# Attention and a gated feed-forward on one core: another written order for the first 19 steps, and 13 casts on VectorE instead of ScalarE

## The chip, the cores and the metric

The kernel runs on one core of a Trainium2 chip. A core has TensorE (PE in the profile), which multiplies matrices into PSUM; VectorE (DVE), ScalarE (ACT) and GpSimd (POOL), which work elementwise; and SyncE (SP), whose queue issues the loads and stores. Each engine works off its own list of instructions in order, and semaphores make one wait for another. The metric is the device time of one execution in microseconds (us), the median of several runs; lower is better.

## The reference

Linear attention over 8 batches of 8 heads with 576 rows of 64 columns, and behind it two matrix products with a nonlinear step between them, all in float32:

```
q_s = softmax(q, over the 64 columns);  k_s = softmax(k, over the 576 rows)
kv  = k_s^T v            (64 x 64, for each batch and head)
x   = q_s kv             -> 4608 x 512
h   = x @ w_in           w_in is 512 x 2048 (float64 words in memory)
g   = h - tanh(h)
out = g @ w_out          w_out is 2048 x 512 (float64 words in memory)
```

## The kernel before

**Two parts for each number.** The products run on float32r operands, a shorter format that TensorE multiplies faster. So each operand is split into a high part (a cast to float32r: xh, gh, the first half of a weight's tile w) and the rest (a subtraction: xl, gl, the second half of w), and a product is three matmuls: high by high, rest by high, high by rest. The change's "casts to the array's format" are the high parts of weights and of g.

**Chunks and steps.** The 4608 rows are nine chunks of 512. For each chunk j and each of the 16 blocks f of the 2048 hidden columns there is a step: 12 matmuls make ph (line 568), and then

- u, t, vv and mk on ScalarE (a square, a tanh, another square and a mask, line 583),
- g, tt, gg and cp on VectorE (lines 589 to 602): they put together h - tanh(h), by a polynomial where h is small,
- gh, the cast of g (line 605, ScalarE), and gl = g - gh (line 608, POOL or VectorE).

Two steps later, 12 matmuls (line 651) multiply gh and gl with w_out's block into four PSUM tiles po; the third of each three reads gl.

The order of steps is: chunk 0 with blocks 0 to 7, chunk 1 with all 16, chunk 0 with blocks 8 to 15, then chunks 2 to 8. Step n has its own names: ph17 is the h block of step 17, chunk 1 and block 9; in listings with numbers it is ph1_9.

**Weights.** Each of the 32 weight blocks (i0 to i15 of w_in, o0 to o15 of w_out) comes as 64-bit words and is turned into two float32r parts: ld (load), cl (a clamp, VectorE, line 157), lo and pr (ScalarE, lines 164 and 161), st (VectorE, line 168, makes c), ca (the cast of c, line 175, ScalarE) and sub (c minus the cast, line 179, VectorE or POOL). All 32 blocks are made within the first 19 steps, beside their h work.

**Attention.** For batch b: k and v loaded (k, v), maxima over rows (km.a to km.d, VectorE, lines 247 to 253; pm, mx, mh, ml, pb bring them to a row and back through TensorE), ks and ke (subtract and exp), pk (matmuls, line 323), sl, rs, rc, kn (norm, giving kvs, line 344). For a tile pair of q: mq, qu, qe, sq, sa, sr (softmax parts, lines 408 to 427), qn (norm, line 447), pt and qs (transpose and copy out), px (matmuls, line 487), xh and xl (lines 506 and 508).

**What sets the order.** Up to step 19 a table of names, ORDER, is worked off in order: each name issues one or a few instructions on its engine, so the table fixes each engine's list for TensorE, VectorE, ScalarE, POOL and SP. A star behind a name gives the piece to VectorE; without one, qu, qn, gl and sub go to POOL. `warm` issues matmuls on an identity whose results nobody reads. From step 19 on a loop issues the steps, TensorE and SP in the loop's order, the others where the scheduler puts them.

```
        for name in ORDER.split():
            eng = (nc.vector,) if name[-1] == "*" else ()
            ...
            if not eng and name.rstrip("0123456789") in ("qu", "qn", "gl") or name[:3] == "sub":
                eng = eng or (nc.gpsimd,)
            ops[name](*eng)
```

Waits between engines follow from who reads and writes which tile. Tiles of ph and of g's parts have two buffers each (vv and mk one), so a later step can also wait for an earlier one to be done with a buffer.

Of the kernel before, what the change touches and what calls it, by code (L numbers as in the profile page):

```python
# [29 lines left out]


ORDER = """
vo0.1 q0 mq0 q1 k0.0 mq1 qu0 k0.1 km0.a qe0 sq0 qu1 k0.2 km0.b sa0 km0.c sr0 qe1 ld.i0 ld.i4
vo0.0 km0.d warm13 pm0 qn0 lo.i4 sq1 lo.i0 mx0 sa1 ld.i2 mh0 sr1 q3 v0.0 ml0 cl.i0 cl.i4 pr.i0
vo0.2 v0.1 v0.2 cl.i2 pr.i2 warm5 pb0 st.i0 pr.i4 ks0.0 ld.i1 ks0.2 lo.i2 qn1 ke0.0 ks0.1 mq3
pt0 qn2 st.i2 qu3* warm4 pt1 ke0.2 ke0.1 st.i4 pk0.0 pk0.1 pk0.2 q2 k1.2 qs0 ca.i0 sl0 rs0 cl.i1
qs1 pt2 ca.i2 qn3 vo1.0 rc0 qe3 lo.i1 kn0 ld.i3 vo1.2 pt3 ld.i5 sub.i2 sub.i0 sq3 qs3 k1.0 pr.i1
qs2 k1.1 mq2 warm2 px0 px2 warm10 xh0.0 xh0.1 st.i1 qu2 xh2.1 ld.o0 xl0.0 xl0.1 xh2.0 xl2.1
ca.i1 xl2.0 ld.o1 lo.i3 cl.i5 qe2 lo.i5 cl.i3 ca.i4 pr.i5 ph0 sa3 pr.i3 sub.i1 u0 ld.i6 sr3 m0
sq2 sa2 km1.a sr2 st.i3 km1.b g0 ld.i7 ph1 km1.c vv0 ca.i3 t0 cl.o0 gg0 u1 pr.o0 km1.d ld.o2 t1  # L40
lo.o0 tt0 cl.o1 vv1 lo.o1 cp0 st.o0 ph2 pm1 sub.i4 mx1 t2 g1 tt1 mh1 qn6 gg1 lo.i6 u2 ca.o0 ml1
st.i5 gh0 m1 vo1.1 v1.0 cp1 vv2 qn4 pt6 ld.i10 sub.i3 qs6 ca.i5 ph3 qn5 t3 gl0 gh1 sub.i5 pb1
ks1.2 ks1.0 m2 v1.1 ld.o3 tt2 gl1 ph4 ks1.1 lo.o2 pt4 g2 ke1.0 u3 ke1.2 cl.i7 gg2 qs4 cl.o2 tt3
ke1.1 u4 vv3 cp2 cl.i6 g3 pr.o1 ld.o5 ph5 st.o1 m3 pr.o2 lo.o3 ca.o1 v1.2 gg3 pr.i6 cl.o3 st.o2
pk1.0 ld.o4 lo.i7 cl.i10 sub.o1* ld.o10 t5 ld.i12 ca.o2 pt5 sub.o0 ld.o6 qs5 pk1.1 cp3 cl.o5 po0
qn7 gh2 pk1.2 sub.o2* st.i6 pr.i7 tt5 t4 sl1 gl2* ld.o12 po1 rs1 ca.i6 g4 sub.i6 tt4 cl.o4 pr.o3
vv4 st.i7 gg4 m4 pt7 cl.o10 lo.o5 gh3 po2 u5 rc1 ca.i7 gl3* qs7 lo.o4 cp4 g5 pr.o5 ld.o9 ph6 m5
pr.o4 kn1 ld.o7 st.o3 px4 cl.o6 vv5 gh4 cl.i12 st.o4 ca.o3 gg5 ca.o4 xh4.1 sub.o3* st.o5 gl4* u6
sub.i7 cp5 xl4.1 xh4.0 cl.o9 t6 ph7 u7 vv6 lo.o7 po3 xl4.0 tt6 t7 px6 ca.o5 gh5 g6 m6 xh6.0
ld.i9 xh6.1 ld.i13 pr.o6 pr.i12 gg6 sub.o4 xl6.0 xl6.1 lo.i10 lo.o6 ld.o8 po4 cl.o12 cl.o7  # L50
sub.o5* cp6 cl.i9 ld.i11 pr.o7 gl5 g7 ph8 st.o6 vv7 lo.i11 m7 ld.i15 tt7 gg7 po5 gh6 pr.i10 cp7
gl6* st.i10 u8 ca.o6 st.o7 ph9 ld.i14 ld.i8 sub.o6* lo.i12 vv8 gh7 g8 po6 pr.i9 t8 lo.i15 t9 u9
tt8 ca.o7 pr.o12 gg8 gl7* m8 sub.o7* vv9 lo.i9 po7.0 cl.i15 cl.i8 pr.i15 tt9 st.i12 cp8 ld.o15
cl.i13 lo.o10 ld.o11 po7.1 ld.o14 gh8 lo.i8 m9 st.i15 ph10 gl8* g9 cl.o15 ev.0 po7.2 cl.i14 sv.0
gg9 ca.i12 u10 cl.o8 cp9 ph11 cl.i11 ev.2 ev.1 t10 ca.i15 vv10 g10 po7.3 tt10 po8.0 m10 sub.i15
cl.o11 cl.o14 po8.1 pr.o10 gg10 t11 gh9 ev.3 u11 ca.i10 gl9* pr.o8 pr.i8 cp10 g11 po8.2 tt11
vv11 m11 sub.i12 ph12 lo.o12 st.o10 gg11 st.i9 sub.i10 ca.o10 t12 lo.o8 lo.o14 st.i8 po8.3 gh10
ph13 cp11 ca.i9 u12 m12 ld.o13 po9 ca.i8 lo.i14 t13 sub.i9* sub.o10* gl10* pr.i11 sv.3 tt12 vv12
g12 st.o12 gh11 gg12 ca.o12 u13 st.i11 pr.o11 gl11* po10 cp12 pr.o9 m13 sub.o12 tt13 vv13 ca.i11
ph14 pr.i14 lo.i13 g13 gg13 po11 sub.i8* u14 sub.i11* cp13 gh12 gl12* t14 st.o8 ph15 lo.o9  # L60
pr.o15 g14 sv.1 po12 m14 gh13 tt14 lo.o11 st.o9 vv14 ca.o8 ph16 gl13* gg14 pr.i13 u15 sv.2 vv15
pr.o14 st.o11 g15 cp14 gh14 t15 sub.o8 lo.o15 u16 po13 m15 gg15 tt15 vv16 t16 cp15 ca.o11 gl14
cl.o13 sub.o11 tt16 g16 ca.o9 st.i14 ph17 gg16 lo.o13 st.i13 gh15 po14 gl15* m16 ca.i14 cp16
ca.i13 u17 g17 ph18 t17 sub.i13* st.o14 vv17 gg17 gh16 ca.o14 tt17 sub.o14* sub.o9* u18 po15
gl16* t18 st.o15 tt18 po16 m17 pr.o13 ca.o15 vv18 st.o13 cp17 gh17 g18 sub.i14 gg18 m18 ca.o13
cp18 gl17* sub.o13* gh18 gl18* sub.o15*
"""


# [1 line left out]
def attn_moe_kernel(  # L71
# [71 lines left out]
    def split_weight(kind: str, f: int) -> dict:

        st = {}

        def words(n: int) -> bass.AP:
            return staged[kind, f].bitcast(U32).rearrange("p (n t) -> p n t", t=2)[:, :, n]

        def clamp():
# [1 line left out]
            nc.vector.tensor_scalar(hif, hif, HI_MAX, -HI_MAX, op0=ALU.min, op1=ALU.max)  # L157
# [8 lines left out]
        def shift():
            st["c"] = c = dec.tile([P, DM], U32, name=f"c_{kind}{f}", tag="c")
            nc.vector.scalar_tensor_tensor(  # L168
                c, words(1), 3, words(0), op0=ALU.logical_shift_left, op1=ALU.bitwise_or
            )  # L170

        def cast():
            del staged[kind, f]
            wt[kind, f] = w = wts.tile([P, 2, DM], F32R, name=f"w_{kind}{f}", tag=f"w{kind}{f}")
            nc.scalar.copy(w[:, 0], st["c"].bitcast(F32))  # L175

        def rest(eng):
            w = wt[kind, f]
            eng.tensor_tensor(  # L179
                w[:, 1], st["c"].bitcast(F32), w[:, 0].bitcast(F32), op=ALU.subtract  # L180
            )
# [391 lines left out]
    def h_parts(j: int, f: int) -> dict:  # L573

        st = {}

# [4 lines left out]
        def act(tag: str, src: str, fn, **kw):
            of = {"dt": kw.pop("dt", F32)} | ({"bufs": kw.pop("bufs")} if "bufs" in kw else {})
            nc.scalar.activation(new(tag, **of), st[src], fn, **kw)  # L583
# [8 lines left out]

        def tt():
            nc.vector.tensor_tensor(st["t"], st["ph"], st["t"], op=ALU.subtract)  # L594

        def gg():
            nc.vector.scalar_tensor_tensor(  # L597
                st["g"], st["vv"], PB, st["g"], op0=ALU.add, op1=ALU.mult
            )

        def cp():
            nc.vector.copy_predicated(st["g"], st["mk"], st["t"])  # L602

        def gh():
            nc.scalar.copy(new("gh", F32R), st["g"])  # L605

        def gl(eng):
            eng.tensor_tensor(  # L608
                new("gl", F32R), st["g"], st["gh"].bitcast(F32), op=ALU.subtract
            )  # L610
# [221 lines left out]
```

## Time and profile before

| | us |
|---|---|
| median of 3 runs (899.38 to 899.83) | 899.44 |
| the profiled execution | 902.51 |
| its span, first to last instruction | 900.7 |
| TensorE busy in the span | 874.9 |
| VectorE busy | 616.7 |
| ScalarE busy | 555.0 |
| GpSimd busy | 289.2 |

The profiled execution is one run with the profiler on; the span is its part from the first to the last instruction. In the rows of the profile, L12 is line 12 of the kernel, `out<-in` are the tiles written and read, `xN` counts instructions, and `<-DVE t L594` behind a number names what ended a wait. A time line's row begins with the start and the length in us. Matmuls are pipelined, so that one that shows 0.39 us can follow the one before after 0.23 us.

### The profile page before, as it was taken

What the parts mean: (1) busy time and instruction counts of PE and PEld (TensorE: products, weight loads), DVE (VectorE), ACT (ScalarE), POOL (GpSimd) and SP (SyncE); (2) the same over time, 40 slices, a digit from 0 to 9 for tenths busy, and PEclk for the clock granted to TensorE, in tenths of its full rate; (3) what the DMA queues carried; (4) which work ended last, traced back from release to release, by engine and by line L of the source; (5) the groups of instructions that cost most, each with busy time, mean ns of one, the idle gap of its engine ahead of it and who ended that gap; (6) DMA issues with size and microseconds to landing.
All of it is one profiled execution on the core that took longest, in us unless ns stands there. A gap on an engine that the chain in (4) does not pass through costs nothing.

```text
span 900.7 us, 13173 instructions
## 1 busy us (share of the span) xinstructions
PE 874.9 (97%) x5008; PEld 716.6 (80%) x5008; DVE 616.7 (68%) x906; ACT 555.0 (62%) x967; POOL 289.2 (32%) x246
## 2 busy tenths in 40 slices
PE   5899989999999999999999999999999999999997
PEld 5777778878778888888888888888888888888886
DVE  7999988957576767567656865866765566454444
ACT  4899986655555657555646565565656566556553
POOL 4631112433144324332333332332433233222221
PEclk8999999999999999999999999999999999999999
DMA  9983301040142202300140011301100020001001
GB/s 292 306 314 118 115 9 41 24 140 2 53 100 61 69 1 82 107 24 1 47 123 7 24 47 35 107 0 48 48 24 1 1 70 12 1 1 48 1 1 47
DMA packets 79775, 57.47 MB, mean 64 GB/s; under 512 B 14688, under 2 KB 72032, under 8 KB 79712
## 3 DMA queue, kind: packets, MB, share of 16 engines
q1 hardware_dynamic: 79712, 56.63, 20.5%
q8 instruction: 39, 0.64, 0.3%
q14 instruction: 24, 0.20, 0.1%
HBM read 46.14 MB, written 10.49 MB: 63 GB/s over the span
## 4 chain that ended last, share of the span: by engine, by line
PE 78%; DVE 12%; ACT 5%; issue 2%; DMA 2%; POOL 1%; SPq 0%; DVEq 0%; ACTq 0%; POOLq 0%
PE po L651 36%; PE ph L568 36%; PE pk L323 2%; PE px L487 2%; PE pt L461 1%; DVE g L589 1%; DMA k<-in_k_dram 1%; DVE t L594 1%; DVE g L597 1%; DVE g L602 1%; ACT gh L605 1%; ACT mk L583 1%; DVE c_o L168 1%; DVE raw_i L157 1%; DVE c_i L168 1%
## 5 line engine op out<-in xcount | busy, mean ns | idle before, releaser
L651 PE MATMUL po<-w_o,gh 128*128 128x512 f32 x1152 | 358.7, 392 | 0.3 <-DVE w_o L179 0.2
L568 PE MATMUL ph<-xh,w_i 128*128 128x512 f32 x1152 | 313.4, 394 | 4.7 <-DVE t L594 2.3
L608 POOL TENSOR_TENSOR gl<-g,gh 128x512 fp32r<-128x512 f32 x128 | 171.5, 1340 | 389.3 <-ACT gh L605 367.0
L568 PEld LDWEIGHTS ph<-xh,w_i 128*128 128x128 f32 x1152 | 213.5, 188 | 49.8 <-DVE t L594 2.8
L651 PEld LDWEIGHTS po<-w_o,gh 128*128 128x128 f32 x1152 | 214.8, 188 | 47.3 <-issue 1.5
L589 DVE SCALAR_TENSOR_TENSOR g<-u,ph 128x512 f32<-128x512 f32 x144 | 98.2, 682 | 209.1 <-ACT t L583 204.7
L651 PE MATMUL po<-w_o,gl 128*128 128x512 f32 x576 | 224.5, 390 | 0.2 <-DVE gl L608 0.2
L605 ACT CAST gh<-g 128x512 fp32r<-128x512 f32 x144 | 89.5, 622 | 176.3 <-DVE g L602 168.5
L568 PE MATMUL ph<-xl,w_i 128*128 128x512 f32 x576 | 155.1, 391 | 0.0
L583 ACT ACTIVATE u<-ph 128x512 f32<-128x512 f32 x144 | 86.1, 598 | 78.4 <-PE ph L568 78.2
L597 DVE SCALAR_TENSOR_TENSOR g<-vv,g 128x512 f32<-128x512 f32 x144 | 117.4, 816 | 18.3 <-ACT vv L583 7.9
L651 PEld LDWEIGHTS po<-w_o,gl 128*128 128x128 f32 x576 | 108.3, 188 | 23.5 <-DVE gl L608 0.7
L568 PEld LDWEIGHTS ph<-xl,w_i 128*128 128x128 f32 x576 | 108.1, 188 | 23.7 <-DVE xl L508 0.5
L602 DVE COPY_PREDICATED g<-mk,t 128x512 f32<-128x512 int32 x144 | 119.6, 830 | 3.4
L583 ACT ACTIVATE mk<-ph 128x512 int32<-128x512 f32 x144 | 86.4, 600 | 36.1 <-DVE g L589 34.2
L583 ACT ACTIVATE vv<-u,b_pa 128x512 f32<-128x512 f32 x144 | 104.8, 727 | 0.7 <-DVE g L597 0.6
L594 DVE TENSOR_TENSOR t<-ph,t 128x512 f32<-128x512 f32 x144 | 98.0, 681 | 6.7 <-ACT mk L583 5.9
L583 ACT ACTIVATE t<-ph 128x512 f32<-128x512 f32 x144 | 85.6, 594 | 3.0 <-DVE g L589 3.0
L447 POOL TENSOR_TENSOR qn<-q,sq 128x512 f32<-128x512 f32 x30 | 34.6, 1153 | 27.7 <-PE pt L461 13.4
L413 POOL TENSOR_TENSOR q<-q,mq 128x1024 f32<-128x1024 f32 x14 | 28.0, 2003 | 46.4 <-DVE mq L408 44.6
L408 DVE TENSOR_REDUCE mq<-q 128x16 f32<-128x1024 f32 x15 | 18.3, 1217 | 23.3 <-DMA q<-in_q_dram 23.3
L179 POOL TENSOR_TENSOR w_i<-c_i,w_i 128x512 fp32r<-128x512 f32 x12 | 18.3, 1529 | 39.1 <-ACT w_i L175 39.1
(94 smaller groups left out, 577.4 us busy)
## 6 DMA issues: line engine op xcount, KB each, us to landing
k<-in_k_dram SPq DMA_DIRECT2D x16, 512.0 KB, 5.5
raw_i<-in_moe_w_in_dram SPq DMA_DIRECT2D x16, 512.0 KB, 6.7
raw_o<-in_moe_w_out_dram SPq DMA_DIRECT2D x16, 512.0 KB, 8.3
...
```

The source lines that it names most:

```text
L179: eng.tensor_tensor(w[:, 1], st["c"].bitcast(F32), w[:, 0].bitcast(F32), op=ALU.subtract)
L413: eng.tensor_tensor(qf, qf, mq, op=ALU.subtract)
L447: eng.tensor_tensor(qn.rearrange("p a g d -> p g a d"), qt[:, :, j].rearrange("p (g a) d -> p g a d", g=2), sq[:, :, j : j + 1] .broadcast ...
L568: nc.tensor.matmul(ph, w[:, i, c], x[:, c, :], start=(n == 0), stop=(n == len(ops) - 1))
L583: nc.scalar.activation(new(tag, **of), st[src], fn, **kw)
L589: nc.vector.scalar_tensor_tensor(new("g"), st["u"], C2, st["ph"], op0=ALU.mult, op1=ALU.mult)
L594: nc.vector.tensor_tensor(st["t"], st["ph"], st["t"], op=ALU.subtract)
L597: nc.vector.scalar_tensor_tensor(st["g"], st["vv"], PB, st["g"], op0=ALU.add, op1=ALU.mult)
L602: nc.vector.copy_predicated(st["g"], st["mk"], st["t"])
L605: nc.scalar.copy(new("gh", F32R), st["g"])
L608: eng.tensor_tensor(new("gl", F32R), st["g"], st["gh"].bitcast(F32), op=ALU.subtract)
L651: nc.tensor.matmul(po[t], g[:, cols], wt["o", f][:, w], start=(begin and n == 0), stop=(end and n == 2),)
```

## The change

The code gets a helper `copy`, and `cast` and `gh` an engine argument, so that a star moves these two kinds of casts to VectorE; the lines below it move down by 3 or 4. ORDER is written anew: the same names, and one more `warm`. Its starred names are 46 instead of 31. One line of the table stands for all here.

```diff
 ORDER = """
-vo0.1 q0 mq0 q1 k0.0 mq1 qu0 k0.1 km0.a qe0 sq0 qu1 k0.2 km0.b sa0 km0.c sr0 qe1 ld.i0 ld.i4
...
+q0 mq0 k0.0 k0.1 qu0* km0.a vo0.0 qe0 k0.2 km0.b km0.c q1 vo1.1 q3 ld.i1 km0.d warm13 pm0 vo0.2
...
 """
...
+    def copy(eng, dst, src):
+        (eng.tensor_copy if eng else nc.scalar.copy)(dst, src)
+
...
-        def cast():
+        def cast(eng=None):
             del staged[kind, f]
             wt[kind, f] = w = wts.tile([P, 2, DM], F32R, name=f"w_{kind}{f}", tag=f"w{kind}{f}")
-            nc.scalar.copy(w[:, 0], st["c"].bitcast(F32))
+            copy(eng, w[:, 0], st["c"].bitcast(F32))
...
-        def gh():
-            nc.scalar.copy(new("gh", F32R), st["g"])
+        def gh(eng=None):
+            copy(eng, new("gh", F32R), st["g"])
```

On VectorE are now the casts of the weights i0, i9, i10, i11, i13, i14, o1, o2 and o7, and gh of steps 6, 7, 9 and 10. Of the other pieces that may be on either engine, VectorE has 15 gl as before, 16 sub (15 before), one qu (q0's; before it was that of the fourth q tile, q3) and one qn (none before); POOL has the others. Behind the planned part the lists of all engines hold the same instructions in the same order as before, save that some stand a place or two apart among their neighbours between steps 19 and 21.

Three places show how the lists move. The first is the start of VectorE's list, up to the first maxima of k. Before:

```order
L408 TENSOR_REDUCE mq0_0_114<-q0_0_112 128x16
L408 TENSOR_REDUCE mq0_1_120<-spare_q_116 128x16
L247 TENSOR_TENSOR km0_125<-k0_0_118 128x512
L421 TENSOR_REDUCE sq0_0_128<-q0_0_112 128x16
L250 TENSOR_TENSOR km0_125<-km0_125,k0_1_123 128x512
L424 TENSOR_SCALAR sq0_0_128<-sq0_0_128 128x16
```

and now:

```order
L412 TENSOR_REDUCE mq0_0_112<-q0_0_110 128x16
L417 TENSOR_TENSOR q0_0_110<-q0_0_110,mq0_0_112 128x1024
L251 TENSOR_TENSOR km0_119<-k0_0_114 128x512
L254 TENSOR_TENSOR km0_119<-km0_119,k0_1_116 128x512 x2
L257 TENSOR_TENSOR km0_119<-km0_119,kr0_124 64x512
L412 TENSOR_REDUCE mq0_1_158<-spare_q_128 128x16
```

The subtraction of q0's maxima (second row) came to VectorE, and the second q tile (spare_q) stands behind all of k's maxima; on SP's list its load moved behind those of k in the same way.

The second place is a moved cast, gh of step 9 (gh1_1: chunk 1, block 1), with its neighbours on VectorE. Before, when gh1_1 was on ScalarE's list:

```order
L157 TENSOR_SCALAR raw_o14_1126<-raw_o14_1126 128x512
L597 SCALAR_TENSOR_TENSOR g1_2_1190<-vv1_2_1188,g1_2_1190 128x512
L608 TENSOR_TENSOR gl1_1_1220<-g1_1_1150,gh1_1_1213 128x512
L602 COPY_PREDICATED g1_2_1190<-mk1_2_1200,t1_2_1184 128x512
L589 SCALAR_TENSOR_TENSOR g1_3_1225<-u1_3_1216,ph1_3_1167 128x512
```

and now:

```order
L598 TENSOR_TENSOR t1_2_1179<-ph1_2_1155,t1_2_1179 128x512
L601 SCALAR_TENSOR_TENSOR g1_2_1177<-vv1_2_1175,g1_2_1177 128x512
L134 CAST gh1_1_1225<-g1_1_1134 128x512
L606 COPY_PREDICATED g1_2_1177<-mk1_2_1189,t1_2_1179 128x512
L612 TENSOR_TENSOR gl1_1_1228<-g1_1_1134,gh1_1_1225 128x512
L161 TENSOR_SCALAR raw_i9_941<-raw_i9_941 128x512
```

The cast stands two places ahead of the gl that reads it, on the same engine.

The third place is the end of the planned part on VectorE, with gl of step 17 (gl1_9) and of step 18 (gl1_10). Before:

```order
L602 COPY_PREDICATED g1_9_1554<-mk1_9_1617,t1_9_1569 128x512
L589 SCALAR_TENSOR_TENSOR g1_10_1629<-u1_10_1584,ph1_10_1556 128x512
L597 SCALAR_TENSOR_TENSOR g1_10_1629<-vv1_10_1622,g1_10_1629 128x512
L602 COPY_PREDICATED g1_10_1629<-mk1_10_1633,t1_10_1600 128x512
L608 TENSOR_TENSOR gl1_9_1638<-g1_9_1554,gh1_9_1627 128x512
L179 TENSOR_TENSOR w_o13_1635<-c_o13_1624,w_o13_1635 128x512
L608 TENSOR_TENSOR gl1_10_1643<-g1_10_1629,gh1_10_1641 128x512
L179 TENSOR_TENSOR w_o15_1620<-c_o15_1602,w_o15_1620 128x512
```

and now:

```order
L606 COPY_PREDICATED g1_9_1584<-mk1_9_1586,t1_9_1550 128x512
L598 TENSOR_TENSOR t1_10_1595<-ph1_10_1567,t1_10_1595 128x512
L601 SCALAR_TENSOR_TENSOR g1_10_1618<-vv1_10_1604,g1_10_1618 128x512
L606 COPY_PREDICATED g1_10_1618<-mk1_10_1625,t1_10_1595 128x512
L183 TENSOR_TENSOR w_i13_1621<-c_i13_1602,w_i13_1621 128x512
L612 TENSOR_TENSOR gl1_10_1632<-g1_10_1618,gh1_10_1630 128x512
L183 TENSOR_TENSOR w_o15_1590<-c_o15_1557,w_o15_1590 128x512
L612 TENSOR_TENSOR gl1_9_1651<-g1_9_1584,gh1_9_1648 128x512
```

Step 17's gl is now the last of the planned part, behind step 18's and the sub of o15; the sub of o13 went to POOL's list.

More of the change, by code (lines that the diff above doesn't have):

```diff
@@ L32 @@
 ORDER = """
-vo0.1 q0 mq0 q1 k0.0 mq1 qu0 k0.1 km0.a qe0 sq0 qu1 k0.2 km0.b sa0 km0.c sr0 qe1 ld.i0 ld.i4
[L34 to L66, printed above, removed]
+q0 mq0 k0.0 k0.1 qu0* km0.a vo0.0 qe0 k0.2 km0.b km0.c q1 vo1.1 q3 ld.i1 km0.d warm13 pm0 vo0.2
+mq1 mx0 ld.i0 mh0 ml0 warm5 pb0 qu1 vo0.1 mq3 v0.0 warm10 sq0 cl.i1 sa0 lo.i1 v0.1 ks0.0 qe1
@@ new lines @@
+lo.i0 pr.i1 sr0 sq1 qu3 ke0.0 ks0.1 cl.i0 v0.2 ld.i4 sa1 qn1 qe3 ks0.2 ke0.1 warm4 pk0.0 sr1 pt1
+qn0 sq3 ke0.2 pk0.1 st.i1 pr.i0 qn3* sa3 pk0.2 lo.i4 cl.i4 sl0 ld.i3 qs1 ld.i2 rs0 qn2 pt0 pt3
+sr3 q2 rc0 warm3 pt2 pr.i4 qs0 ca.i1 kn0 cl.i3 ld.i5 st.i0 qs3 qs2 px0 xh0.0 sub.i1* k1.0 xh0.1
+ca.i0* px2 cl.i2 xh2.0 xh2.1 qn7 xl0.0 lo.i3 xl0.1 lo.i2 k1.1 xl2.0 xl2.1 pr.i2 sub.i0 k1.2
+pr.i3 warm2 pt7 warm2 ph0 lo.i5 mq2 st.i2 ph1 ca.i2 cl.i5 pr.i5 st.i4 ca.i4 st.i3 sub.i2* km1.a
+ca.i3 st.i5 u0 ld.o2 t0 g0 ca.i5 vv0 km1.b tt0 ld.o0 ld.o1 km1.c u1 gg0 m0 km1.d cp0 qn6 ph2 pm1
@@ new lines @@
+g1 mx1 t1 vv1 gg1 mh1 cl.o0 qu2 vo1.2 qe2 ld.i7 u2 ml1 lo.o0 sub.i3 sq2 gh0 tt1 ph3 cl.o1 m1 qs7
+vo1.0 lo.o1 sa2 pr.o0 vv2 pb1 lo.o2 v1.2 sub.i5 cp1 st.o0 sub.i4 pr.o1 t2 ph4 sr2 pt6 gh1 ks1.0
+ks1.1 v1.0 gl0 u3 m2 ke1.0 v1.1 ks1.2 ph5 t3 g2 tt2 ke1.1 qs6 pk1.0 ca.o0 gl1 qn4 ld.i6 ke1.2
+gg2 g3 vv3 ld.o3 cp2 ld.o6 tt3 pk1.1 st.o1 cl.o2 ca.o1* m3 u5 pt4 t5 ld.o4 gg3 ld.o5 pk1.2 sl1
+qs4 cl.i6 cl.o3 pr.o2 st.o2 u4 cl.i7 pr.i6 ca.o2* qn5 rs1 pr.o3 sub.o0 lo.i6 ld.i10 po0 gh2 pt5
+ld.o7 cl.o6 qs5 cp3 ld.o10 rc1 st.i6 kn1 gl2* sub.o2* cl.o5 ld.o8 cl.o4 lo.o3 t4 tt5 g4 ld.o11
@@ new lines @@
+sub.o1 tt4 po1 m4 ca.i6 ld.i12 gh3 pr.i7 pr.o4 st.o3 lo.i7 ld.i8 lo.o4 vv4 st.o4 gg4 ca.o3
+sub.i6 sub.o3* gl3* st.i7 px4 cp4 xh4.1 xh4.0 ca.o4 vv5 lo.o5 po2 ld.i15 ph6 pr.o6 xl4.1 u6
+xl4.0 ca.i7 g5 m5 lo.o6 ld.o9 sub.i7* gg5 gh4 st.o6 pr.o5 gl4* st.o5 po3 px6 cp5 ld.i9 xh6.0
+xh6.1 ph7 xl6.1 ld.i11 t6 ld.i13 ca.o5 m6 sub.o4 ca.o6 g6 tt6 lo.i12 gh5 xl6.0 po4 t7 gl5* vv6
+cl.o7 u7 lo.o7 ld.o12 cl.i10 cl.i12 gg6 cl.i8 ld.o13 lo.i8 cp6 tt7 pr.o7 gh6* g7 vv7 gg7 sub.o5
+gl6* lo.i15 ph8 st.o7 sub.o6 m7 cp7 po5 u8 ph9 ca.o7* vv8 gh7* lo.i9 gl7 pr.i8 t8 lo.o9 lo.i10
@@ new lines @@
+g8 pr.i12 m8 po6 u9 tt8 gg8 pr.i10 sub.o7* po7.0 cp8 ld.o14 cl.o8 cl.i11 po7.1 po7.2 t9 gh8
+st.i12 st.i8 lo.o12 gl8* ca.i8 g9 st.i10 lo.o8 cl.o13 pr.i11 ca.i10* po7.3 cl.i15 ev.2 vv9
+lo.i13 tt9 m9 ph10 cl.i13 gg9 cp9 u10 pr.o8 cl.o12 vv10 g10 t10 sub.i10* tt10 ev.3 po8.0 gg10
+m10 ph11 t11 po8.1 ph12 u11 gh9* cp10 gl9* cl.i9 ev.1 lo.o14 ev.0 g11 po8.2 m11 vv11 ld.i14
+ca.i12 lo.i11 st.o8 t12 tt11 gg11 pr.i9 tt12 ca.o8 cl.o14 pr.o12 po8.3 ph13 po9 gh10* lo.i14
+cp11 pr.o13 u12 cl.i14 cl.o10 cl.o9 sv.1 pr.o9 sub.i8 gl10* u13 sv.2 g12 st.i11 lo.o11 m12
@@ new lines @@
+sub.o8* sub.i12 gh11 vv12 st.o12 pr.o10 st.i9 po10 gg12 t13 ph14 cp12 m13 pr.i14 ca.i11* pr.i15
+gl11* vv13 ca.i9* ca.o12 g13 tt13 gh12 u14 sub.i9* gg13 sub.o12* pr.o14 po11 cl.o11 st.i15
+ld.o15 vv14 cp13 m14 gh13 st.o14 sv.0 t14 ph15 lo.o13 ca.i15 gl12* sub.i11 st.o9 gl13 tt14
+ca.o14 g14 lo.o15 t15 sub.i15* gg14 po12 pr.i13 ph16 cp14 u15 m15 vv15 st.o13 g15 gh14 ca.o13
+sub.o14 tt15 pr.o11 po13 u16 gl14* cl.o15 gg15 st.i14 g16 ph17 po14 lo.o10 ca.o9 sub.o9* t16
+ca.i14* cp15 pr.o15 vv16 st.o11 ca.o11 t17 u17 gh15 sub.i14* st.o15 tt16 gg16 m16 gl15* cp16
@@ L67 @@
+sub.o13 ph18 st.o10 vv17 g17 m17 gh16 ca.o15 ca.o10 gg17 t18 gl16* sub.o10* u18 st.i13 vv18 po15
+g18 tt17 ca.i13* cp17 tt18 m18 gg18 cp18 sub.i13* gh18 gl18* sv.3 sub.o15* po16 gh17 sub.o11
+gl17*
 """
```

## The prediction

> **What bounds the kernel now.** I read the page first, then the engines' busy time stage by stage, then the waits of TensorE (PE) and VectorE (DVE), and last the time lines at the places where they meet.
>
> ```profile
> PE 874.9 (97%) x5008; PEld 716.6 (80%) x5008; DVE 616.7 (68%) x906; ACT 555.0 (62%) x967; POOL 289.2 (32%) x246
> ```
>
> The page says TensorE, but a busy TensorE isn't one at its peak. The count of matmuls (the x) in equal stretches of 20 us tells more; the last three columns are the granted clock, the DMA share and GB/s.
>
> ```profile
> 40.00:60.00 20.00, 17.94 (x154) 14.40 (x155) 19.67 (x34) 18.27 (x33) 9.94 (x6) 1.00 1.07 363
> 60.00:80.00 20.00, 18.61 (x134) 14.29 (x134) 19.22 (x35) 18.91 (x38) 5.42 (x4) 1.00 0.24 83
> 80.00:100.00 20.00, 19.48 (x84) 15.24 (x83) 18.65 (x35) 19.19 (x37) 0.00 (x0) 1.00 0.41 150
> 100.00:120.00 20.00, 19.45 (x86) 15.74 (x86) 17.82 (x27) 18.38 (x35) 5.45 (x4) 1.00 0.37 119
> 120.00:140.00 20.00, 17.66 (x71) 14.11 (x70) 17.00 (x27) 17.45 (x33) 5.47 (x4) 0.91 0.00 0
> 140.00:160.00 20.00, 20.00 (x90) 16.54 (x89) 17.69 (x28) 12.10 (x23) 2.50 (x4) 1.00 0.21 47
> 400.00:420.00 20.00, 20.00 (x120) 16.25 (x119) 16.55 (x24) 12.12 (x21) 5.78 (x4) 1.00 0.10 27
> ```
>
> From about 140 us on TensorE is busy all the time. Up to there VectorE and ScalarE are 85 to 98% busy and TensorE waits for them now and then. So the planned part is bound by those two, the rest by TensorE, and **what the planned part gains or loses by its last step goes into the end one for one**. The waits confirm it: the longest one behind the start of the first h block is
>
> ```profile
> PE ph L568 <- DVE t L594: 2.3, 1, 2.3
> ```
>
> ```profile
> 134.94 4.33 PE ph L568 x12
> ...
> 142.32 2.72 PE ph L568 x12
> ```
>
> and behind it, in the chain of waits, twelve matmuls take 4.33 us where they take 2.72 a little later: the granted clock (0.91 in that stretch) fell with the wait. The point where VectorE hands over to TensorE is the product po, whose third matmul reads gl:
>
> ```profile
> 63.66 0.50 PE L651 MATMUL po<-w_o,gl 128*128 128x512 f32 x1 [0.22 <-DVE gl L608]
> ```
>
> ```profile
> 150.70 0.68 DVE L608 TENSOR_TENSOR gl<-g,gh 128x512 fp32r<-128x512 f32 x1
> ```
>
> ```profile
> 153.50 0.39 PE L651 MATMUL po<-w_o,gl 128*128 128x512 f32 x1
> ```
>
> (The first and the last row are TensorE's, the middle one VectorE's.) At 63.66 it waits. The gl of step 17, ready at 151.38, is read at 153.50: a slack of 2.1 us only. That step is my yardstick, since it is the last gl that VectorE makes in the changed order.
>
> **The change, part by part.**
>
> *Casts.* 13 casts leave ScalarE.
>
> ```profile
> L175 ACT CAST w_i<-c_i 128x512 fp32r<-128x512 f32 x16 | 10.1, 631 | 1.4 <-DVE c_i L168 1.4
> L605 ACT CAST gh<-g 128x512 fp32r<-128x512 f32 x144 | 89.5, 622 | 176.3 <-DVE g L602 168.5
> L179 DVE TENSOR_TENSOR w_o<-c_o,w_o 128x512 fp32r<-128x512 f32 x11 | 7.5, 685 | 0.8 <-ACT w_o L175 0.8
> ```
>
> ```profile
> 69.79 0.43 DVE L157 TENSOR_SCALAR raw_o<-raw_o 128x512 f32<-128x512 f32 x1
> 70.13 0.42 DVE L157 TENSOR_SCALAR raw_i<-raw_i 128x512 f32<-128x512 f32 x1
> 70.51 0.69 DVE L168 SCALAR_TENSOR_TENSOR c_o<-raw_o 128x512 uint32<-128x512 uint32 x1
> 71.12 0.69 DVE L597 SCALAR_TENSOR_TENSOR g<-vv,g 128x512 f32<-128x512 f32 x1
> ```
>
> ```profile
> 70.88 0.64 ACT L605 CAST gh<-g 128x512 fp32r<-128x512 f32 x1
> 71.39 1.17 ACT L175 CAST w_o<-c_o 128x512 fp32r<-128x512 f32 x2
> ```
>
> Instructions overlap, so the price is from start to start: a cast on ScalarE 0.51 us (70.88 to 71.39), thirteen 6.7 us. On VectorE no such cast of this size is in the trace. The nearest row with one input from SBUF is the clamp, 0.34 (69.79 to 70.13); the nearest with two is 0.61 (70.51 to 71.12). A cast has one input, so I take 0.34: 13 x 0.34 = **+4.4 us on VectorE**, at most 13 x 0.61 = 7.9. The Trainium skill, VectorE: DVE Perf Modes, section "The perf-mode tier table", gives fp32 copies out of SBUF twice the rate of two-input operations; the clamp row agrees, and at the single rate the sum would be the 7.9.
>
> *Two more pieces on VectorE.* One more sub (16 for 15) and one qn come from POOL: 2 x 0.61 = **+1.2**. qu takes part on VectorE for another q tile, once in either order.
>
> *Order at the end.* Before, three instructions of the planned part stood behind step 17's gl on VectorE (the gl of step 18, the subs of o13 and o15); now none does, all of VectorE's planned work is ahead of it: 3 x 0.61 = **+1.8**. Together 7.4 us more work stand ahead of the yardstick.
>
> *What hides it.* VectorE isn't full:
>
> ```profile
> 44.70:150.70 106.00, 97.75 (x162) 0.98 0.38 128
> ```
>
> ```profile
> DVE t L594 <- ACT mk L583: 4.1, 5, 2.2
> DVE w_i L179 <- ACT w_i L175: 1.4, 1, 1.4
> DVE w_o L179 <- ACT w_o L175: 0.8, 3, 0.4
> DVE t L594 <- ACT t L583: 0.7, 1, 0.7
> ```
>
> Of 106.00 us it idles 8.2, and these four waits for ScalarE are 7.0 of it. ScalarE loses 6.7 us, and four weights get cast and subtracted on VectorE alone. So I let 6.2 us of the idle time be filled and keep 2.0 (a cast whose result the next instruction reads costs some): **-6.2**, with bounds of 0 and -8.2. If this cover is gone, the 7.4 us are late in full.
>
> *Collisions.* A second loss is no idle time in the profile:
>
> ```profile
> 72.64 1.29 POOL L179 TENSOR_TENSOR w_o<-c_o,w_o 128x512 fp32r<-128x512 f32 x1 [3.32 <-ACT w_o L175]
> 72.69 1.80 DVE L168 SCALAR_TENSOR_TENSOR c_o<-raw_o 128x512 uint32<-128x512 uint32 x1
> ```
>
> ```profile
> 165.86 1.30 POOL L608 TENSOR_TENSOR gl<-g,gh 128x512 fp32r<-128x512 f32 x1 [1.84 <-issue]
> ```
>
> ```profile
> 165.92 1.26 DVE L268 CAST mh<-mx 128x4 fp32r<-128x4 f32 x1
> ```
>
> The c that takes 0.69 at 70.51 takes 1.80 beside a POOL operation, and a cast of four columns takes 1.26: VectorE is held until POOL has ended. The new casts can be held likewise. The Trainium skill, SBUF — State Buffer, section "Who interferes with whom", says so and speaks against this change: a cast or copy in the two-port mode and a GpSimd operation lock each other out, whole instructions long; the mh row agrees. In price: POOL is busy 16.3 of 80 us (60 to 140), so of 13 casts 2.7 would meet it and lose half of 1.3 us each, 1.7 us. Against it two POOL operations go, each worth up to 1.3 us. I take **0**, with bounds of -2.6 and +2.5.
>
> *The start.* The written order of the first 45 us changes most: k's tiles are loaded ahead of the second q tile, q0's subtraction is VectorE's, and the second batch's k comes earlier.
>
> ```profile
> 7.77 1.90 POOL L413 TENSOR_TENSOR spare_q<-spare_q,mq 128x1024 f32<-128x1024 f32 x1
> ```
>
> ```profile
> 7.81 2.41 DVE L247 TENSOR_TENSOR km<-k 128x512 f32<-128x512 f32 x1 [0.49 <-DMA k<-in_k_dram]
> ```
>
> ```profile
> 27.50 1.21 DVE L408 TENSOR_REDUCE mq<-q 128x16 f32<-128x1024 f32 x1
> 28.63 0.68 DVE L168 SCALAR_TENSOR_TENSOR c_i<-raw_i 128x512 uint32<-128x512 uint32 x1
> 29.23 2.47 DVE L508 TENSOR_TENSOR xl<-px,xh 128x512 fp32r<-128x512 f32 x4
> ```
>
> ```profile
> 30.77 1.17 PE L568 MATMUL ph<-xh,w_i 128*128 128x512 f32 x4
> 31.78 1.18 PE L568 MATMUL ph<-xl,w_i 128*128 128x512 f32 x4
> ```
>
> The first h block is held by the last xl, ended at 31.70. VectorE's work ahead of it changes by: + qn 0.61, + sub of i1 0.61, + cast of i0 0.34, + one clamp 0.34, - one row maximum of q 1.13 (27.50 to 28.63), - two c of 0.61: -0.5 us. The km that lost 1.8 us beside POOL at 7.81 is free of it now, as q0's subtraction is VectorE's, but mh and the clamps come to stand beside two q subtractions of 1.90 on POOL instead, with k1's maxima beside a third. I take **-0.7**, bounds -2.0 and +2.0.
>
> *Sum.* +4.4 +1.2 +1.8 -6.2 +0 -0.7 = +0.5: step 17's gl is ready at 151.9 instead of 151.4. Nothing says that TensorE must be where it was: before, it was pushed to 153.50 by the wait at 132 to 135 and the slow clock behind it. If VectorE is what it follows, it reads gl at once, at 151.9: 1.6 us before 153.50. All that follows (POOL's and ScalarE's work for the next batches, SP's loads behind the planned ones) stands in the same order as before, under a TensorE without gaps. The forecast is **-1.6 us**.
>
> **The rivals.**
> - *VectorE fills up* (slower). Its idle time is pinned to TensorE's h tiles and to short chains, so only 2.0 us instead of 6.2 close. For it: VectorE is the fuller of the two up to 80 us, and work goes to it. Against it: 7.0 us of idle are ScalarE's doing. +4.2: end +2.6, 902.0. It decides from 4.6 us of idle left: there the 2.1 us of slack are used up.
> - *Dear casts* (slower). At 0.61 each +3.5: end +1.9, and with half the price of the lock 902.2. Against it stands the clamp row.
> - *The start and the meetings with POOL go well* (faster). The start gives 2.0, collisions fall by 2.2: 3.5 better, end -5.1, 894.3. For it: km's 1.8 us are avoided. Against it: POOL's list is hardly shorter.
> - *It doesn't do what it says.* ScalarE's relief only makes ScalarE wait, VectorE's gaps and load cancel, and TensorE's waits stay: 899.4.
>
> **How the numbers follow.** The profiled execution took 902.51 us, 1.8 more than its span of 900.7, and is 3.1 above the median of the runs, 899.44. I carry the shift to the median: 899.44 - 1.6 = **897.9**. About 0.2% (1.8 us) is what a measurement here can tell from no change, so the bounds are 897.6 and 901.2. Forecast: chance 0.45, own range 895.5 to 900.5 (0.21 faster, 0.24 same). VectorE full: 0.22 (0.19 slower, 0.03 same). Dear casts: 0.07 slower. Start well: 0.18 faster. No effect: 0.08 same. Faster 0.39, same 0.35, slower 0.26. The range takes in the rivals' centres and a little more, 893.5 to 903.5; with several bounds at once (collisions +2.5 and no idle time filled, or the start -2.0, collisions -2.6 and all of it filled) it could be 906.6 or 892.0.
>
> **What would show it.** Right: casts on line L134 of VectorE start 0.34 apart from their followers; VectorE's idle time between 45 and 150 falls from 8.2 to about 2; step 17's gl ends near 152 and TensorE waits for it; the clock has no dip near 134. Wrong: VectorE still idles 5 us or more there; casts of 1 us and over beside POOL; the first h block later than 31.5; or TensorE waiting for something other than VectorE (a weight's cast on ScalarE, or a load) in that stretch.

## The result and the profile after

The changed kernel takes 909.56 us (median of 3 runs, 909.32 to 910.11) against 899.44 before: 1.0101 times as long, 95% interval 1.0087 to 1.0115. The forecast was 897.9, range 893.5 to 903.5. The profiled execution took 910.11 us with a span of 908.3, 7.6 more than before; the medians are 10.1 us apart, since the profiled execution of before lay 3.1 us above its median and this one 0.6. In the profiles TensorE is 7.6 us late from step 25 on (ph0_9, 196.0 instead of 188.4) and stays so to the end. At step 17's gl, in the last steps of the planned part, it is 8.4 us late (161.86 instead of 153.50): all of the loss is made there.

The page's line of busy times, and then the engines' busy time in stretches of 20 us (PE, PEld, DVE, ACT, POOL with counts; granted clock, DMA share, GB/s), of the changed kernel:

```profile
PE 880.2 (97%) x5018; PEld 719.3 (79%) x5018; DVE 623.8 (69%) x921; ACT 548.6 (60%) x954; POOL 286.6 (32%) x244
```

(TensorE has ten rows more than before because the new table has two more `warm` entries, `warm3` and a second `warm2`, and not one: five products of two rows each.)

```profile
40.00:60.00 20.00, 16.23 (x138) 13.43 (x139) 18.95 (x27) 14.68 (x26) 9.36 (x7) 0.83 1.00 361
60.00:80.00 20.00, 16.80 (x98) 12.09 (x96) 16.64 (x32) 15.38 (x29) 4.60 (x3) 1.00 0.61 218
80.00:100.00 20.00, 18.41 (x105) 14.33 (x103) 17.78 (x33) 17.85 (x33) 3.85 (x3) 1.00 0.09 27
100.00:120.00 20.00, 18.62 (x79) 14.53 (x80) 18.91 (x36) 17.13 (x32) 2.60 (x2) 1.00 0.25 80
120.00:140.00 20.00, 19.50 (x86) 15.85 (x85) 19.60 (x31) 16.62 (x31) 4.74 (x3) 1.00 0.21 60
140.00:160.00 20.00, 17.73 (x77) 14.01 (x76) 18.84 (x31) 12.71 (x24) 3.12 (x4) 1.00 0.21 47
```

Against the same stretches of before, VectorE did less between 40 and 80 us (35.6 us busy, 38.9 before) and ScalarE fell by 7.1 us (30.1, 37.2 before) where it gave away two casts, those of o1 and o2. In 60 to 80 us TensorE began 98 matmuls instead of 134. So the engines that bind this part stand idle where they had been full.

The prediction's yardstick, VectorE up to the end of step 17's gl: 151.38 us before, 161.80 now, where TensorE waits for it. The first row is VectorE's (time line of the changed kernel), the second TensorE's:

```profile
161.12 0.68 DVE L612 TENSOR_TENSOR gl<-g,gh 128x512 fp32r<-128x512 f32 x1
```

```profile
161.86 0.50 PE L655 MATMUL po<-w_o,gl 128*128 128x512 f32 x1 [0.68 <-DVE gl L612]
```

Split into busy and idle time, by VectorE's rows alone of the view of stretches (length of the stretch, busy time and count; then the granted clock, the DMA share and GB/s). Before:

```profile
20.00:44.70 24.70, 24.56 (x38) 1.00 0.93 302
44.70:151.40 106.70, 98.44 (x163) 0.98 0.38 127
```

and after:

```profile
20.00:44.70 24.70, 24.63 (x40) 0.94 0.83 263
44.70:161.80 117.10, 107.81 (x183) 0.98 0.37 126
```

The 10.4 us are 9.4 of busy time (98.44 to 107.81) and 1.0 of idle time (8.26 to 9.29). The prediction had 6.7 more busy time and 6.2 less idle time.

**Where VectorE idles now.** Its three costliest waits for others between 30 and 165 us (us in total, times, longest):

```profile
DVE c_o L172 <- ACT raw_o L168: 3.4, 1, 3.4
DVE t L598 <- ACT mk L587: 1.5, 1, 1.5
DVE t L598 <- ACT t L587: 0.9, 1, 0.9
```

The longest seen from both sides, in the time lines. ScalarE:

```profile
66.21 0.58 ACT L587 ACTIVATE t<-ph 128x512 f32<-128x512 f32 x1
70.33 0.60 ACT L587 ACTIVATE mk<-ph 128x512 int32<-128x512 f32 x1 [3.54 <-DVE t L598]
...
73.52 0.65 ACT L168 ACTIVATE raw_o<-raw_o 128x512 uint32<-128x512 uint32 x1
```

VectorE:

```profile
69.56 0.68 DVE L598 TENSOR_TENSOR t<-ph,t 128x512 f32<-128x512 f32 x1
70.16 0.68 DVE L172 SCALAR_TENSOR_TENSOR c_o<-raw_o 128x512 uint32<-128x512 uint32 x1
74.20 0.69 DVE L172 SCALAR_TENSOR_TENSOR c_o<-raw_o 128x512 uint32<-128x512 uint32 x1 [3.36 <-ACT raw_o L168]
```

ScalarE has t of step 4 done at 66.79 and could make the mask mk of the same step, but waits until VectorE's tt of step 4 has ended at 70.24. The mask takes nothing from tt: what the two have in common is that they read the same ph. Two readers of a ph take turns, in the order that the table gives (`tt4 po1 m4`). The Trainium skill, PSUM — Partial Sum Buffer, section "PSUM bank collisions raise a hardware error", gives a reason: two engines must not access the same partitions of one bank at once, and the compiler's scheduler puts a dependency between any two such accesses, reads against reads included. The wait of 3.54 us here agrees with it; no run here shows a collision. After 70.33 it is VectorE's turn to stand idle: the next piece of its list, c of o4, needs lo of o4, which stands on ScalarE behind the mask and five more instructions. So one pair of names costs both engines over 3 us one after the other.

The pair itself is not new. The table of before has the five readers of step 4's ph in the same order, `tt4` ahead of `m4`, and there the mask waited 0.27 us. ScalarE, before:

```profile
62.49 0.57 ACT L583 ACTIVATE t<-ph 128x512 f32<-128x512 f32 x1
65.03 0.60 ACT L583 ACTIVATE mk<-ph 128x512 int32<-128x512 f32 x1 [0.27 <-DVE t L594]
```

Between t and mk the old list had three other pieces for ScalarE (the cast of i6, pr of o3 and vv of step 4); the new list has none, and puts six behind the mask, lo of o4 the last of them. What changed is what stands around the turn.

**Where VectorE is held.** A second place is the row maxima of batch 1. VectorE and then POOL, of the changed kernel:

```profile
36.75 1.77 DVE L254 TENSOR_TENSOR km<-km,k 128x512 f32<-128x512 f32 x1
38.44 0.68 DVE L598 TENSOR_TENSOR t<-ph,t 128x512 f32<-128x512 f32 x1
39.04 1.17 DVE L254 TENSOR_TENSOR km<-km,k 128x512 f32<-128x512 f32 x1
40.13 1.75 DVE L601 SCALAR_TENSOR_TENSOR g<-vv,g 128x512 f32<-128x512 f32 x1
41.80 1.74 DVE L257 TENSOR_TENSOR km<-km,kr 64x512 f32<-64x512 f32 x1
```

```profile
32.33 5.63 POOL L417 TENSOR_TENSOR q<-q,mq 128x1024 f32<-128x1024 f32 x1 [1.46 <-DVE mq L412]
...
37.98 1.68 POOL L183 TENSOR_TENSOR w_i<-c_i,w_i 128x512 fp32r<-128x512 f32 x1
...
39.67 3.33 POOL L183 TENSOR_TENSOR w_i<-c_i,w_i 128x512 fp32r<-128x512 f32 x2
```

Four rows of 1.17 to 1.77 us where an undisturbed one is 0.68, each ending 0.5 to 0.6 us behind the end of an instruction of POOL. Before, two of the rows here were held (1.53 at 36.64 and 1.18 at 38.70). TensorE's transposes of the maxima wait for them,

```profile
PE pm L263 <- DVE km L257: 4.4, 1, 4.4
```

and the granted clock is 0.83 in the stretch that holds this wait.

**The casts** cost what was forecast. Behind the first cast shown the next instruction starts 0.33 us after it, and 12 of the 13 take 0.41 to 0.43:

```profile
60.45 0.41 DVE L134 CAST w_o<-c_o 128x512 fp32r<-128x512 f32 x1
60.78 0.68 DVE L601 SCALAR_TENSOR_TENSOR g<-vv,g 128x512 f32<-128x512 f32 x1
...
125.76 1.53 DVE L134 CAST w_i<-c_i 128x512 fp32r<-128x512 f32 x1
```

The exception stands beside a subtraction on POOL (125.38 to 127.01).

### The profile page after: what moved, and what is told of

The parts are those of the page before. It is cut to its first block, busy times and chain, and to the rows that moved or that the text cites. A ratio compares the mean times of both kernels' runs of the same rounds, so it can differ in the third digit from the quotient of the medians.

```text
span 908.3 us, 13193 instructions
## 1 busy us (share of the span) xinstructions
PE 880.2 (97%) x5018; PEld 719.3 (79%) x5018; DVE 623.8 (69%) x921; ACT 548.6 (60%) x954; POOL 286.6 (32%) x244
## 4 chain that ended last, share of the span: by engine, by line
PE 79%; DVE 12%; ACT 4%; issue 2%; DMA 1%; SPq 0%; POOL 0%; DVEq 0%; ACTq 0%; POOLq 0%
PE po L655 37%; PE ph L572 36%; PE pk L327 2%; PE px L491 2%; DVE g L601 1%; PE pt L465 1%; DVE g L606 1%; DVE g L593 1%; DVE t L598 1%; DVE c_i L172 1%; DVE raw_i L161 1%; DMA spare_q<-in_q_dram 1%; DVE c_o L172 1%; DVE gl L612 1%; ACT mk L587 1%
## 5 line engine op out<-in xcount | busy, mean ns | idle before, releaser
L134 ACT CAST gh<-g 128x512 fp32r<-128x512 f32 x140 | 86.7, 620 | 175.4 <-DVE g L606 172.0
L417 POOL TENSOR_TENSOR q<-q,mq 128x1024 f32<-128x1024 f32 x14 | 31.4, 2246 | 43.2 <-DVE mq L412 43.2
L451 POOL TENSOR_TENSOR qn<-q,sq 128x512 f32<-128x512 f32 x30 | 32.4, 1081 | 26.2 <-PE pt L465 14.1
L512 DVE TENSOR_TENSOR xl<-px,xh 128x512 fp32r<-128x512 f32 x36 | 23.7, 678 | 1.2 <-ACT xh L510 1.2
```

Of the source, the lines that this page charges most:

```text
L134: (eng.tensor_copy if eng else nc.scalar.copy)(dst, src)
L417: eng.tensor_tensor(qf, qf, mq, op=ALU.subtract)
L451: eng.tensor_tensor(qn.rearrange("p a g d -> p g a d"), qt[:, :, j].rearrange("p (g a) d -> p g a d", g=2), sq[:, :, j : j + 1] .broadcast ...
L512: nc.vector.tensor_tensor(xl, px_of[i][g], xh.bitcast(F32), op=ALU.subtract)
```

## Experiments

Three theories: **L** (load: VectorE can't carry the 13 casts), **T** (turns: the new order makes VectorE and ScalarE wait for each other's reads of ph), **C** (collisions of VectorE with POOL). All kernels of the list compute the whole reference. The ratio sets the executions of a kernel against those of the kernel before that ran beside them on the same chip (its medians there: 900.77 to 901.31, 1.3 to 1.9 us above the 899.44 that the expectations reckon from). It is not quite the quotient of the two medians, and kernels are compared by it; the changed kernel stands at 1.0101.

| kernel | median us | ratio to before, 95% interval |
|---|---|---|
| e1 new order, 13 casts back on ScalarE | 914.28 | 1.0146 [1.0130, 1.0162] |
| e2 old order, 13 casts on VectorE | 905.19 | 1.0041 [1.0025, 1.0056] |
| e3 changed, t1 and m4 earlier | 905.61 | 1.0052 [1.0037, 1.0067] |
| e4 changed, three subs on VectorE | 908.26 | 1.0082 [1.0066, 1.0099] |
| e5 e3 + e4 + m8 earlier | 901.80 | 1.0013 [1.0003, 1.0022] |
| e6 old order, t15 and m15 earlier | 899.20 | 0.9984 [0.9975, 0.9994] |
| e7 old order, 12 casts on VectorE | 902.07 | 1.0019 [1.0009, 1.0028] |
| e8 e5, six late casts back | 902.69 | 1.0019 [1.0010, 1.0028] |
| e9 changed, m4 earlier alone | 905.32 | 1.0053 [1.0037, 1.0068] |
| e10 e5 + m1 earlier | 901.52 | 1.0001 [0.9990, 1.0013] |
| e11 e6 + cast of i9 on VectorE | 898.92 | 0.9977 [0.9965, 0.9989] |
| e12 e5, 13 casts back | 907.66 | 1.0077 [1.0064, 1.0091] |

### The casts and the order apart: e1 and e2

e1 takes the stars from the 13 casts in the new table; e2 sets them in the old one:

```diff
-ca.i0* ... ca.o1* ... ca.o2* ... gh6* ... ca.o7* ... gh7* ...
+ca.i0 ... ca.o1 ... ca.o2 ... gh6 ... ca.o7 ... gh7 ...
```

> The changed kernel with the 13 casts given back to ScalarE, each at its place in the new order. Theory L (load): VectorE sets the end of the planned part and the 13 casts at 0.34 us are what it cannot carry; 13 x 0.34 = 4.4 us go from it, and the time falls from 909.6 to about 905. Theory T (turns): the new order makes VectorE and ScalarE wait for each other in the middle (3.36 us of VectorE at 74.2, 5.05 and 3.54 us of ScalarE at 44.8 and 70.3); those stay, ScalarE gets 13 x 0.5 = 6.5 us more beside 34 us of idle time, and the time stays within 908 to 912. Theory C (collisions): the stretched VectorE rows at 36 to 44 us set the loss there; no cast of the 13 stands there on VectorE, so the time stays at 908 to 911.

> The order of before with the same 13 casts given to VectorE, each at its place in that order, and nothing else. Theory L: VectorE gets 4.4 us more where it had 8.2 us idle, 7.0 of them waiting for ScalarE; if its load alone decides, the time rises from 899.4 to about 903 to 904. Theory T: the order is at fault and not the casts; they take 6.5 us from ScalarE, which VectorE waited for, and the time is between 896 and 900. Theory C: 898 to 901.

e1 came out against all three theories, L by its sign, T and C as the loss is larger than they gave. The new order alone costs 1.46%, some 13 us, and **the casts on VectorE give 4 us of it back**. VectorE up to the end of step 17's gl in e1, same view as above:

```profile
44.70:165.16 120.46, 103.92 (x171) 0.97 0.35 119
```

Idle 16.54 us against 9.29 with the casts on VectorE: they add 3.9 us of work (13 x 0.34 is 4.4) and close 7.25 of idle time. Where they close it shows in e1's time lines; VectorE:

```profile
98.50 0.69 DVE L591 SCALAR_TENSOR_TENSOR g<-u,ph 128x512 f32<-128x512 f32 x1 [2.81 <-ACT t L585]
100.65 0.69 DVE L596 TENSOR_TENSOR t<-ph,t 128x512 f32<-128x512 f32 x1 [1.47 <-ACT mk L585]
```

and ScalarE, where the cast of o7 and then gh of step 7 stand in the way of t:

```profile
95.11 0.62 ACT L132 CAST w_o<-c_o 128x512 fp32r<-128x512 f32 x1 [0.49 <-DVE c_o L170]
...
96.26 0.60 ACT L132 CAST gh<-g 128x512 fp32r<-128x512 f32 x1
...
97.89 0.57 ACT L585 ACTIVATE t<-ph 128x512 f32<-128x512 f32 x1
```

In the old order the same casts cost 0.41% (seven executions, 902.12 to 905.74; the profile is of the longest). There the first h block came at 33.2 instead of 30.8, behind a cast of i0 that POOL held up:

```profile
23.58 1.52 DVE L132 CAST w_i<-c_i 128x512 fp32r<-128x512 f32 x1
```

In e7, without this one cast on VectorE, it is at 29.7.

### The turns and the collision apart: e3, e4 and e9

```diff
-ph2 pm1 g1 mx1 t1 ... t4 tt5 g4 ... tt4 po1 m4
+ph2 pm1 t1 g1 mx1 ... t4 m4 tt5 g4 ... tt4 po1
```

for e3; e9 has the move of m4 alone; e4 gives the subs of i3, i4 and i5 a star.

> The changed kernel with two names of the table moved: t1 ahead of g1, and m4 right behind t4 (ahead of g4 and tt4). ScalarE then need not wait 5.05 us for VectorE's g of step 1 and 3.54 us for tt of step 4. Theory T: lo of o4 comes some 3 us sooner, VectorE's gap of 3.36 us at 74.2 goes, and most of it reaches the end: 905.5 to 907.5. Theory L: the end is set by VectorE's own sum, but a gap less is as good as work less, so 906 to 907 too if the gap is not made up elsewhere; if ScalarE's new head start only makes VectorE wait elsewhere, 909 to 910. Theory C: nothing before 44 us changes, so ph of step 3 stays at 44.4 and the loss up to there (2.0 us) stays.

> The changed kernel with the subtractions of i3, i4 and i5 on VectorE instead of GpSimd, at their places. Theory C: GpSimd then has no elementwise work at 38 to 43 us, so the stretched rows of VectorE (km1 1.17 and 1.74, g 1.75 where 0.68 is a lone one) go back by some 2.6 us, against 3 x 0.60 = 1.8 us of added work, two of the three behind km1's last row: pm of batch 1 comes 1.5 to 2.5 us sooner, and the time is 907 to 909. Theory L: 1.8 us more on VectorE: 911 to 912. Theory T: 909 to 911.

> The changed kernel with one name moved: m4 right behind t4, nothing else. Theory T1 (this one turn carries what the two turns brought together): ScalarE's wait of 3.54 us at 70.3 and VectorE's of 3.36 us at 74.2 go, ph of step 7 comes some 4 us sooner, and the time is 905.0 to 906.2, as with both turns (905.6). Theory T2 (both turns count): 906.5 to 908.

e3 is 0.5% faster than the changed kernel, and e9 as much: **the one name m4 carries all of it, 4.3 us** (1.0101 to 1.0053). ScalarE in e9:

```profile
65.94 0.59 ACT L585 ACTIVATE t<-ph 128x512 f32<-128x512 f32 x1
66.42 0.59 ACT L585 ACTIVATE mk<-ph 128x512 int32<-128x512 f32 x1
```

The mask now starts 0.48 us behind t, and the c of o3 and of o4 follow each other on VectorE without a gap:

```profile
69.87 1.28 DVE L170 SCALAR_TENSOR_TENSOR c_o<-raw_o 128x512 uint32<-128x512 uint32 x2
```

The turn of t1, the longer wait of ScalarE (5.05 us), brought nothing that the intervals could show: in e3 ScalarE waits 4.21 us a little later, for tt of step 1, so the wait was moved and not ended. VectorE waited 0.6 us behind the one and 0.9 us behind the other.

e4 did at its place what theory C says, VectorE's rows there:

```profile
38.75 0.68 DVE L252 TENSOR_TENSOR km<-km,k 128x512 f32<-128x512 f32 x1
39.35 0.68 DVE L599 SCALAR_TENSOR_TENSOR g<-vv,g 128x512 f32<-128x512 f32 x1
39.95 0.68 DVE L255 TENSOR_TENSOR km<-km,kr 64x512 f32<-64x512 f32 x1
```

Three of the four held rows are back at 0.68 us, and batch 1's pm starts at 40.7 instead of 43.6. The time is 0.2% less; the intervals of e4 and of the changed kernel overlap, so this gain alone isn't shown.

### Together: e5, e10 and e12

e5 has e3's two moves, `m8` right behind `t8`, and e4's three stars; e10 also has `m1` right behind `t1`; e12 is e5 with all 13 casts back on ScalarE.

> The changed kernel with three turns moved (t1 ahead of g1, m4 right behind t4, m8 right behind t8) and the subtractions of i3, i4 and i5 on VectorE. The two earlier runs gave -4.4 us for the first two turns and -1.7 us for the subtractions, against the changed kernel, by their ratios. Theory T+C (both act, at different places): 909.6 - 4.4 - 1.7 - 1.4 (VectorE's gap of 1.48 us at 98.1, which m8 opens) = 902.1. Theory L (one sum on VectorE, and a gap opened is filled by the next wait): the sum is smaller than its parts, 904 to 906.

> The kernel e5 (three turns and the three subtractions) with m1 right behind t1, too. ScalarE then does not wait 3.78 us at 47.7 for VectorE's tt of step 1. Theory L (VectorE's sum decides, and a wait of ScalarE counts only where VectorE waits behind it): behind this wait VectorE stands idle 0.62 us at 49.9 (c_o0) at most, so 901.2 to 901.9, the same as e5 (901.8) or 0.6 us less. Theory T (every wait of ScalarE for a turn reaches the end): 898 to 900.

> The kernel e5 with all 13 casts back on ScalarE. In the changed kernel giving them back cost 4.0 us, and VectorE then waited 2.81 and 1.46 us for ScalarE at 98 to 101 us and 3.30 at 75. Theory T (these waits come from turns, which e5 has mended): giving them back costs 0 to 1.5 us, 901.8 to 903.5. Theory S (with the new order ScalarE has too much to do at 55 to 105 us, whatever the turns): the casts back cost 3 us or more again, 905 to 907.

By the ratios e5 gains 0.88% on the changed kernel, 7.9 us, where its parts added up to 7.5 (4.4 and 1.7 from e3 and e4, and 1.4 for m8, an estimate that no run has alone). Each part is uncertain by 1 us and more, so the costs add as far as these runs can tell, and L's 904 to 906 is out. VectorE in e5 to the same point:

```profile
44.70:155.15 110.45, 105.98 (x180) 0.98 0.34 114
```

Idle 4.47 us. e10 can't be told from e5 (1.1 us less by the ratios, 0.3 by the medians). That is in line with L, by which a wait of ScalarE counts only if VectorE waits behind it, but the intervals still allow the 1.8 us at which T's range begins. e12 bears out the number of its theory S, which T, C and L lacked: with the turns mended, giving the casts back costs 0.6%, 5.8 us, and VectorE idles 12.30 us again:

```profile
44.70:159.47 114.77, 102.47 (x170) 0.99 0.36 118
```

So the new order needs the casts on VectorE, in its first form (4.0 us) and in its mended one (5.8). That ScalarE simply has too much to do at 55 to 105 us is not shown: in these 50 us it is busy 44.9 in e12, 45.9 in e5 and 46.5 in the kernel before. What the time lines of e1 show is casts that stand in front of t and mk on ScalarE's list, with VectorE waiting behind those.

### The old order once more: e6, e7, e11, and the late casts: e8

```diff
-g15 cp14 gh14 t15 sub.o8 lo.o15 u16 po13 m15 gg15 tt15
+g15 cp14 t15 m15 gh14 sub.o8 lo.o15 u16 po13 gg15 tt15
```

for e6; e11 adds a star to `ca.i9`; e7 is e2 without the star on `ca.i0`.

> The kernel before with one place of its order changed: t15 and m15 ahead of gh14. VectorE's gap of 2.19 us at 134.2 (tt of step 15 waits for the mask of step 15, which stands on ScalarE behind gh of step 14, which waits for VectorE) goes. Theory T (a turn on ScalarE in the middle of VectorE's work is paid in full): TensorE waits less there and its clock does not fall behind it, 895.5 to 898. Theory L or C: the gap is at the end of VectorE's work, where TensorE is the bound from 134.9 on, so 899 to 900.

> The order of before with twelve of the thirteen casts on VectorE; the cast of i0 stays on ScalarE. With all thirteen the start was 2.4 us late (first h block at 33.2 instead of 30.8, the cast of i0 took 1.52 us beside GpSimd), and then nothing was lost up to 100 us. Theory C (the cost of the casts in the old order is one stretched cast at the start): the first h block is back at 30.8 and the time at 899 to 901. Theory L: twelve casts still cost 4.0 us, 903.

> The kernel e6 (the order of before with t15 and m15 ahead of gh14) with one of the 13 casts on VectorE, that of i9. VectorE there stands idle 1.44 us at 110.5 for ScalarE's cast of i9. Theory T+L (a cast on VectorE pays where it ends a wait of VectorE that is longer than the cast): 0.34 us instead of 1.44, so 1.1 us less than e6, 898.1. If the wait is made up behind it anyway: the same as e6, 899.2, within 0.4.

> The kernel e5 with the six late casts (gh of steps 9 and 10, i9, i11, i13, i14) back on ScalarE. Theory L: VectorE is the bound from 115 to 161 us and ScalarE idle for 11 us there, so 6 x 0.34 = 2.0 us less than e5. Theory T: each cast that goes back makes VectorE wait for ScalarE again, so the same as e5 within 0.8 us, as the milestones behind 107 us showed when all thirteen went back.

e6 is 0.16% faster than before: the wait that the prediction had shown at 132 to 135 goes (VectorE's longest wait there is 0.7 us, 2.2 before), and with it 1.4 us by the ratio, 1.6 by the medians (899.20 beside 900.78). That is the edge of what theory T gave, 1.4 to 3.9, and more than the nothing of L and C. e7 loses 0.19%, just above what C gave and well below L: less than with the cast of i0, though the two intervals still overlap by 0.03%. Its VectorE,

```profile
44.70:152.64 107.94, 101.93 (x172) 1.00 0.37 123
```

has 3.5 us more work than before and 2.25 less idle time: in the old order twelve casts find too little idle time that they can close, even with a start 1.1 us earlier. e11 can't be told from e6 (the intervals overlap); it is faster than before by 0.23% (0.11 to 0.35), and in it VectorE's wait of 1.44 us for the cast of i9 has become a cast of 0.40. e8 equals e5 within the intervals: six late casts cost the same on either engine, and not the 2.0 us that L gave.

## Why the prediction was wrong

- *TensorE bound by VectorE up to the yardstick, and reading it at once*: right. It waited 0.68 us for step 17's gl and read it at 161.86.
- *Casts +4.4*: right in size (0.33 to 0.34 us each; +3.9 between e1 and the changed kernel). One of 13 was held by POOL, 1.1 us; half the price of the lock for 2.7 of them had been weighed.
- *Idle time -6.2*: **this is the step that failed.** The prediction took VectorE's 8.2 us of idle time from the old order and let the casts fill them. That they fill such time was right: between e1 and the changed kernel 7.25 us closed. But the idle time to be filled wasn't the old one: the same rows in the new order without the casts show 16.54. The sum had terms for the work that the new table moves, and none for the waits that it makes: idle time came out 1.0 us up and not 6.2 down, and one such wait, ended by moving m4 alone, was worth 4.3 us. The turn of `tt4` and `m4` stood in both tables, and the pair alone does not tell its price; it cost 0.27 us in the old one, where ScalarE had three pieces between t and mk, and 3.54 in the new one, where it has none. The trace of before had shown the kind of wait, t or mk of ScalarE waiting for tt or g; the prediction weighed only the places that it had listed.
- *Start -0.7*: wrong in sign. The first h block came as before (30.7), but the last row of batch 1's maxima ended at 43.54 and not, as before, at 41.42: +2.1. The prediction named the maxima beside POOL's q subtraction, and gave the start bounds of -2.0 and +2.0; the three subs behind it on POOL's list were not in it. Work pushed behind 44.7 us by it is in the busy time, which came out 2.7 us above the sum; idle time came out 7.2 above: together the 9.9 us by which the yardstick missed (10.4 against 0.5).
- *Collisions 0*: too low, within its bounds. Counted over VectorE's rows that took at least 0.2 us more than an undisturbed one of their kind, the excess up to the yardstick was 12.9 us in 16 rows before and 15.0 us in 17 rows now: +2.1, of which 1.7 lie behind 44.7 us and make up most of the 2.7 us of busy time above the sum. e4 shows some 3 us at one place, ahead of the yardstick's window.
- *-1.6 carried to the median*: a second, smaller fault. Of the 2.1 us of slack at 153.50 some 1.4 came from the slow clock behind the wait at 134 (4.33 us for twelve matmuls that take 2.9 in e7). The profiled execution lay 3.1 us above the median, and e7 shows a wait of 2.0 us at the same place with the clock at 1.00 (last section). The median runs may not have had that slack to give; how many had, no run here shows.
- *Rival "VectorE fills up"*: nearest, with the sign right and the reason wrong. It had the idle time pinned to h tiles, closing by 2.0; it grew by 1.0, from the order, and e5 with three names and three stars moved leaves 4.47 of it. Its threshold was misreckoned, too: the slack of 2.1 us is used up when 4.6 us of the 8.2 are filled, so with 3.6 us of idle time left and not with 4.6.
- *Signs named ahead*: casts 0.34 apart, as forecast; "VectorE still idles 5 us or more" came true, and so did a weight's cast among TensorE's waits (0.8 us for w_o on ScalarE); no dip of the clock near 134, but one at 40 to 60.

A check of this account is e10, which, with turns and collision mended, equals before to within 0.1%. The sum of its parts on VectorE (4.4 + 1.2 + 1.8 and the three subs, 1.8, less 4.4 of idle time) would put its yardstick 4.8 us later; it was at 153.52, 2.1 later. The rest, 2.7, is about what its held rows have less than those of before: 10.0 us in 11 rows against 12.9 in 16, counted as above. What stays open is why other rows are held from kernel to kernel, and what each place costs in the median runs: each kernel has one trace.
